# The second FFN product of each unit by Strassen's scheme, with 256-column matmuls and sums on GpSimd

## The chip, the cores and the metric

The kernel runs on one core of a Trainium2 chip. A core has a matrix engine (TensorE, PE in the profile), three engines for elementwise work (VectorE or DVE, ScalarE or ACT, GpSimd or POOL) and a queue that issues DMAs (SyncE or SP). Each engine works through its own list of instructions in order and waits on semaphores for the others. Only PE, DVE and ACT reach the accumulators (PSUM banks); POOL works on SBUF alone. The metric is the time of one execution on the device, in microseconds; lower is better.

## The reference

The inputs are q, k and v of 8 sequences, 8 heads, 576 positions and 64 features, a layer norm's gain and two FFN weights. Attention is local, in chunks of 64 positions; its output, brought to 4608 rows of 512 features, goes through a layer norm and an FFN with a residual:

```python
scores = scale * np.matmul(q_c, k_c.transpose(0, 1, 2, 4, 3))
attn = np.exp(scores - np.max(scores, axis=-1, keepdims=True))
attn = attn / (np.sum(attn, axis=-1, keepdims=True) + 1e-09)
out = np.matmul(attn, v_c)
...
xn = (x - mu) / np.sqrt(var + 1e-06) * g_ln
ch = np.maximum(xn @ w_ch1, 0.0) @ w_ch2
return x + ch
```

## The kernel before, in words

The 4608 rows are 18 pairs of 256 rows, or 9 tiles of 512. The first three tiles (pairs 0 to 5) go through attention and a plain FFN while the weights are read, rounded and split. The other six tiles form three units of two tiles (1024 rows), and a unit's FFN is `unit_ffn`.

*Precision.* Each float32 operand is split into a high part (fp32r, written by ScalarE) and a low part (the difference, by DVE or POOL). A product is three matmuls: high x high, high x low, low x high. So `m` runs over three terms everywhere.

*First product of a unit* (512 to 2048 features). It is done by Strassen's scheme: the unit's two tiles and two halves of the features give seven combinations of activations (`operand`, made by `combine`), and the weights seven combinations that `prepare` writes to DRAM (`wa`). Per quarter `q` of the hidden features there are 14 steps (seven products for two `e`), each `product` six matmuls of 512 columns (line 778). The four PSUM banks of `ps_y` hold two accumulators per `e`, `c_` and `a_`. After most steps something leaves a bank: ScalarE copies it to a snapshot or to `hu` (line 784), or DVE adds the bank and a snapshot into `hu` (line 787). `hu` holds the unit's hidden values, 2 x 16 blocks of 128 x 512.

*Second product of a unit* (2048 back to 512). It is plain: for each of the two tiles `n` and 16 blocks `f`, 12 matmuls of 512 columns (line 863: four groups of rows `j` by three terms), accumulated over `f` in four banks. Ahead of them, `split` has ScalarE write the rectified high part (line 800) and `rest` has DVE write the low part (line 805). At the end DVE adds the residual (line 903) and SP stores the rows.

*Weights.* A ring of six buffers of 512 KB each is loaded by SP (line 687): 28 loads per unit of `wa` and 32 of `w2d` (the second weight, written plainly to DRAM by `prepare`).

*Order.* Every engine's list is written out by hand. Up to the units the order comes from strings and tables of tokens: `START`, `SECOND`, `THIRD`, where one letter is one step of a stream (`S` is a step of `prepare`, `P` and `Q` are `combine` of the two halves for the first unit). In the units, `weave` counts the matmuls of 512 columns that `unit_ffn` has issued (0.2267 us each) and lets in steps of the next unit's attention and of `combine` at given counts (`PAIR_SPAN`, `STEPS`, `FIRST_HALF`, `LAST_HALF`). Attention of a pair has two blocks of small matmuls on PE (lines 298 and 387), transposes of 32 x 32 blocks on DVE (lines 358 and 467) and reductions, scalings and statistics on DVE and ScalarE. In `combine`, `part` has ScalarE write an operand's high part (line 730) and POOL its low part (line 731), and `less` subtracts on DVE (line 734).

*Preparation* (`prepare`). For each of eight pairs of weight blocks: POOL adds the high and low parts of the first weight together (line 635), makes four combinations of 256 columns (lines 643 to 646), ScalarE copies the high parts (line 655), POOL subtracts them (line 657), and SP writes all to DRAM; five steps per pair of blocks.

Of the kernel before, what the change touches and what calls it, by code (L numbers as in the profile page):

```python
# [44 lines left out]
    0: "CS", 1: "CS", 2: "DDGS", 3: "DS", 4: "DDS", 5: "DS", 6: "DGS", 7: "GGHS", 8: "DG", 9: "D", 10: "GGP",  # L45
    11: "HGGP", 12: "G", 13: "G", 14: "GGHP", 15: "GHP", 16: "GHP", 17: "GP", 18: "HHGP", 19: "HGP", 20: "HGP",
# [4 lines left out]
PAIR_SPAN = 140  # L51
LOADED = 8
STEPS = (0, 6, 11, 18, 26, 37, 48, 59, 68, 76, 88, 95, 102, 110, 118, 129, 140, 158)
ONE_STEP = 9
FIRST_HALF = 345
LAST_HALF = 592
REST = (2, 6, 20)
# [15 lines left out]
RING = 6  # L73

# [23 lines left out]
def chunk_attention_ffn(ctx: ExitStack, tc: tile.TileContext, qkv, v01, g, w, out):  # L98
# [527 lines left out]
    w2d = [dram.tile([P, 2, DM], F32, name="w2d", tag=f"w2d{f}") for f in range(NF)]  # L626

    def prepare():
        late = []
        for p in range(NF // 2):  # L630
            fe, q, e = 2 * p, p // 2, p % 2
            both = [wp[fe], wp[fe + 1]]
            t_ = raws.tile([P, 2, 2, PAIR], F32, name="sums", tag="wf")
            for i in range(2):
                nc.gpsimd.tensor_tensor(
                    out=t_[:, i], in0=both[i][:, 0, :DM].rearrange("p (a n) -> p a n", a=2).bitcast(F32),
                    in1=both[i][:, 1, :DM].rearrange("p (a n) -> p a n", a=2).bitcast(F32), op=ALU.add,
                )
            for i in range(2):
                nc.sync.dma_start(w2d[fe + i], both[i][:, :, DM:].bitcast(F32))  # L640
            yield
            a11, a12, a21, a22 = t_[:, 0, 0], t_[:, 0, 1], t_[:, 1, 0], t_[:, 1, 1]
            nc.gpsimd.tensor_tensor(out=a22, in0=a21, in1=a22, op=ALU.add)
            nc.gpsimd.tensor_tensor(out=a21, in0=a11, in1=a21, op=ALU.subtract)
            nc.gpsimd.tensor_tensor(out=a11, in0=a22, in1=a11, op=ALU.subtract)
            nc.gpsimd.tensor_tensor(out=a12, in0=a12, in1=a11, op=ALU.subtract)
            for to, of in late:
                nc.sync.dma_start(to, of.bitcast(F32))
            nc.sync.dma_start(wa[q][:, e, 0], both[0][:, :, PAIR:DM].bitcast(F32))
            nc.sync.dma_start(wa[q][:, e, 1], both[0][:, :, :PAIR].bitcast(F32))  # L650
            nc.sync.dma_start(wa[q][:, 6, e], both[1][:, :, PAIR:DM].bitcast(F32))
            yield
            yield
            r = raws.tile([P, 2, 2, 2, PAIR], F32R, name="parts", tag="raw")
            nc.scalar.copy(r[:, 0], t_)
            yield
            nc.gpsimd.tensor_tensor(out=r[:, 1], in0=t_, in1=r[:, 0].bitcast(F32), op=ALU.subtract)
            late = [
                (wa[q][:, 2 + e, 0], r[:, :, 0, 0]), (wa[q][:, 4 + e, 1], r[:, :, 0, 1]),
                (wa[q][:, 4 + e, 0], r[:, :, 1, 0]), (wa[q][:, 2 + e, 1], r[:, :, 1, 1]),  # L660
            ]
            yield
        for to, of in late:
            nc.sync.dma_start(to, of.bitcast(F32))
        yield

    class Ring:
# [10 lines left out]
        def fetch(self):  # L678
            if self.given < len(self.loads):
                place = self.places[self.given % RING]  # L680
                of = self.loads[self.given]
                to = place[:, : 2 * DM].bitcast(F32)
                if len(of.shape) == 4:
                    to = to.rearrange("p (i h n) -> p i h n", i=2, h=2)
                else:
                    to = to.rearrange("p (h n) -> p h n", h=2)
                nc.sync.dma_start(to, of)
                self.given += 1
# [8 lines left out]
    for _ in range(UNITS):  # L697
        for q in range(NF // 4):
            ring.loads.extend(wa[q][:, i] for i in range(7))
        ring.loads.extend(w2d[f][:, :, :] for _ in range(2) for f in range(NF))  # L700
# [17 lines left out]
    def operand(name):  # L718
        if name not in shared:
            shared[name] = const.tile([P, 2, 2, 2 * PAIR], F32R, name="xc", tag=f"w{'2165734'.index(name)}")  # L720
        return shared[name]

    def combine(half):
# [4 lines left out]
        def part(name, x):  # L728
            o = operand(name)[:, :, :, cs].rearrange("p h k (j t) -> p h k j t", j=2)
# [11 lines left out]
        yield  # L741
        less(b12, b22, b12)
        yield
        part("3", b22)
        yield
        less(b22, b22, b11)
        yield
        part("6", b22)
        yield
        part("5", b11)  # L750
        yield
        less(b21, b21, b22)
        yield
        part("7", b12)
# [4 lines left out]
    def unit_ffn(u):  # L759
        first = 2 * LEAD + 4 * u  # L760
        tail = u == UNITS - 1
        hu = {}
        for n in range(2):
            for f in range(NF):
                if f // 2 not in hu:
                    hu[f // 2] = shared.setdefault(
                        f"h{f // 2}", None
                    ) or const.tile([P, 2, 2, DM], F32, name="hu", tag=f"w{8 + f // 2}")
                    shared[f"h{f // 2}"] = hu[f // 2]
# [3 lines left out]
        def product(bank, w, name, start):  # L773
            x = operand(name)
# [14 lines left out]
        more = []  # L789
        order = [(n, f) for n in range(2) for f in range(NF)]  # L790
        parts = []

        def split(i):
            n, f = order[i]
            if i % 5 > 1:
                hh, hl = more[i % 5 - 2][:, 0], more[i % 5 - 2][:, 1]
            else:
                hh, hl = (hp_.tile([P, 1, DM], F32R, name=f"h{c}")[:, 0] for c in "hl")
            x = hu[f // 2][:, n, f % 2]
            nc.scalar.activation(hh, x, AF.Relu)  # L800
            parts.append((hh, hl, x))

        def rest(i):
            hh, hl, x = parts[i]
            nc.vector.scalar_tensor_tensor(  # L805
                out=hl, in0=x, scalar=0.0, in1=hh.bitcast(F32), op0=ALU.max, op1=ALU.subtract
            )

        for q in range(NF // 4):
# [8 lines left out]

            steps = []
            for e in range(2):  # L820
                steps += [
                    (c_, e, "2", None),
                    (a_, e, "1", lambda e: (copy(s[e][0], a_[e]), add(h[e][:, 0, 0], c_[e], s[e][0]))),
                ]
            for e in range(2):
                steps += [
                    (a_, e, "6", lambda e: copy(s[e][1], a_[e])),
                    (c_, e, "5", lambda e: copy(s[e][2], c_[e])),
                ]
            for e in range(2):  # L830
                steps += [
                    (a_, e, "7", lambda e: add(h[e][:, 1, 1], a_[e], s[e][2])),
                    (c_, e, "3", lambda e: add(h[e][:, 1, 0], c_[e], s[e][1])),
                ]
            for e in range(2):
# [193 lines left out]
```

## Time and profile before

| | |
|---|---|
| time, median of 3 runs | 845.76 us (845.73 to 846.2) |
| the profiled execution | 846.09 us, of which the span from the first to the last instruction is 844.3 us |
| granted TensorE clock | 0.999 |
| units start at | 326.5, 502.0 and 677.4 us |
| busy in the span | PE 831.7, weight loads 682.0, DVE 561.4, ACT 270.8, POOL 151.5 us |
| DMA | 192.6 MB, mean 228 GB/s |

Durations of a row are of a single instruction; the engines overlap the end of one with the start of the next, so that the start-to-start distance can be shorter than the duration (PE: 391 ns long, 227 ns apart). A group's row names line, engine, operation, output and inputs, shape and count, then busy time and mean duration in ns, then the idle time of the engine before them and what ended it. A row of the order of time begins with start and length in us.

### The profile page before, as it was taken

To read this page: it belongs to the slowest core of one execution; us is meant where nothing else is said; L and a number is where in the kernel's file an instruction comes from. 1 tells how busy PE (TensorE), PEld (TensorE's weight loads), DVE (VectorE), ACT (ScalarE), POOL (GpSimd) and SP (SyncE) were. 2 spreads that over 40 slices of the span, in tenths; PEclk is the share of its full clock that TensorE was granted. 3 is DMA by queue.
4 is the path that set the end of the run, shared out by engine and by line. 5 is a ranking of instruction groups with operands and counts; after the bars stand their busy time and mean duration, and the time that the engine had idled before them with its cause. 6 is when DMAs were issued, how large, how long until landed. Compare 5 with 4: busy or idle time off the path is not lost.

```text
span 844.3 us, 14613 instructions
## 1 busy us (share of the span) xinstructions
PE 831.7 (99%) x5850; PEld 682.0 (81%) x5850; DVE 561.4 (66%) x957; ACT 270.8 (32%) x425; POOL 151.5 (18%) x138
## 2 busy tenths in 40 slices
PE   7999999999999999999999999999999999999998
PEld 4888888888888888888787888887878888888886
DVE  6989966787556736797999927879999421232321
ACT  5766431122322333222341402324223212232220
POOL 0111006473751223000130400001302300000000
PEclk9999999999999999999999999999999999999999
DMA  9997417938982147776786868877658776667572
GB/s 363 328 274 221 157 43 239 345 142 286 324 270 79 42 175 259 230 257 200 254 312 208 291 190 296 276 217 254 236 192 276 243 248 188 192 195 246 189 281 106
DMA packets 69043, 192.60 MB, mean 228 GB/s; under 512 B 6640, under 2 KB 20976, under 8 KB 67056
## 3 DMA queue, kind: packets, MB, share of 16 engines
q1 hardware_dynamic: 67680, 186.95, 64.1%
q0 software_dynamic: 1296, 4.72, 2.9%
q8 instruction: 46, 0.75, 0.3%
q14 instruction: 21, 0.17, 0.1%
HBM read 147.08 MB, written 39.85 MB: 221 GB/s over the span
## 4 chain that ended last, share of the span: by engine, by line
PE 84%; DVE 11%; DMA 2%; issue 1%; ACT 1%; SPq 0%; POOL 0%; ACTq 0%; DVEq 0%; POOLq 0%
PE y L778 24%; PE y L863 17%; PE y L551 15%; PE h L527 15%; PE h L863 8%; DVE pt_sb L358 3%; DVE rows L467 2%; PE s L298 2%; DMA wp<-wfs 1%; PE h L387 1%; DVE hx L805 1%; DVE top L305 1%; DMA k_t<-qkv 1%; PE s L387 1%; DVE hu L787 1%
## 5 line engine op out<-in xcount | busy, mean ns | idle before, releaser
L778 PE MATMUL y<-xc,ring 128*128 128x512 f32 x1008 | 232.5, 391 | 0.4 <-DVE hu L787 0.4
L778 PEld LDWEIGHTS y<-xc,ring 128*128 128x128 f32 x1008 | 188.3, 188 | 40.6 <-DVE hu L787 1.2
L527 PE MATMUL h<-xth,wp 128*128 128x512 f32 (+1 forms) x432 | 129.6, 370 | 1.1 <-DMA wp<-wfs 1.1
L863 PE MATMUL y<-ring,hx 128*128 128x512 f32 x486 | 128.0, 391 | 0.0
L863 PEld LDWEIGHTS y<-ring,hx 128*128 128x128 f32 x486 | 90.8, 188 | 19.0
L787 DVE TENSOR_TENSOR hu<-y,snap 128x512 f32<-128x512 f32 x72 | 49.2, 690 | 82.8 <-ACT snap L784 43.2
L551 PE MATMUL y<-wp,hh 128*128 128x512 f32 x376 | 96.2, 394 | 0.0
L527 PEld LDWEIGHTS h<-xth,wp 128*128 128x128 f32 x432 | 78.2, 188 | 15.9 <-DMA wp<-wfs 1.3
L784 ACT COPY snap<-y 128x512 f32<-128x512 f32 x72 | 42.2, 586 | 121.2 <-PE y L778 121.2
L731 POOL TENSOR_TENSOR xc<-rows,xc 128x512 fp32r<-128x512 f32 x42 | 58.7, 1413 | 123.8 <-ACT xc L730 119.8
L551 PEld LDWEIGHTS y<-wp,hh 128*128 128x128 f32 x376 | 69.1, 188 | 13.9
L358 DVE STREAM_TRANSPOSE pt_sb<-p_sb 32x256 f32<-32x256 f32 x176 | 76.7, 436 | 3.5 <-ACT p_sb L333 0.5
L527 PE MATMUL h<-xtl,wp 128*128 128x512 f32 (+1 forms) x216 | 78.3, 367 | 0.0
L541 DVE SCALAR_TENSOR_TENSOR hl<-h,hh 128x512 fp32r<-128x512 f32 (+1 forms) x53 | 33.0, 629 | 64.9 <-ACT hh L540 64.7
L863 PE MATMUL y<-ring,hh 128*128 128x512 f32 x252 | 68.9, 389 | 0.0
L467 DVE STREAM_TRANSPOSE rows<-xg 32x256 f32<-32x256 f32 x144 | 62.7, 436 | 5.4 <-ACT xg L449 3.2
L540 ACT ACTIVATE hh<-h 128x512 fp32r<-128x512 f32 (+1 forms) x53 | 28.5, 546 | 117.7 <-PE h L527 117.7
L805 DVE SCALAR_TENSOR_TENSOR hx<-hu,hx 128x512 fp32r<-128x512 f32 x54 | 43.9, 817 | 30.2 <-PE y L863 12.2
L863 PEld LDWEIGHTS y<-ring,hh 128*128 128x128 f32 x252 | 47.3, 188 | 9.9
L551 PE MATMUL y<-wp,hl 128*128 128x512 f32 x188 | 51.8, 390 | 0.0
L437 POOL TENSOR_TENSOR rstd<-vare,mhalf 128x2 f32<-128x2 f32 x12 | 10.6, 886 | 229.5 <-DVE vare L436 229.5
L863 PE MATMUL h<-ring,hx 128*128 128x512 f32 x162 | 49.9, 389 | 0.0
(130 smaller groups left out, 986.6 us busy)
## 6 DMA issues: line engine op xcount, KB each, us to landing
ring<-w2d SPq DMA_DIRECT2D x96, 512.0 KB, 4.3
ring<-wa SPq DMA_DIRECT2D x84, 512.0 KB, 4.3
raw<-w SPq DMA_DIRECT2D x15, 1024.0 KB, 7.3
out<-x SPq DMA_DIRECT2D x36, 256.0 KB, 4.5
q_t<-qkv SPq DMA_DIRECT2D x17, 512.0 KB, 5.8
k_t<-qkv SPq DMA_DIRECT2D x17, 512.0 KB, 6.8
v_t<-qkv SPq DMA_DIRECT2D x32, 256.0 KB, 6.8
w2d<-wp SPq DMA_DIRECT2D x16, 512.0 KB, 7.1
```

The costliest lines, as they stand in the source:

```text
L358: nc.vector.transpose(out=pt_sb[quad(2 * h2 + j), :, c, quad(i)], in_=p_sb[quad(2 * c + i), :, h2, quad(j)])
L467: nc.vector.transpose(out=to[quad(j), :, quad(i)], in_=of[quad(i), :, quad(j)])
L527: nc.tensor.matmul(h, lhsT=(wh, wh, wl)[m][:, ks], rhs=(xth, xtl, xth)[m][:, k, :], start=i == 0, stop=i == len(terms) - 1,)
L540: nc.scalar.activation(hh, h, AF.Relu)
L541: nc.vector.scalar_tensor_tensor(out=hl, in0=h, scalar=0.0, in1=hh.bitcast(F32), op0=ALU.max, op1=ALU.subtract)
L551: nc.tensor.matmul(sums(pairs[j // 2])[j % 2], lhsT=(hh, hh, hl)[m], rhs=(wh, wl, wh)[m], start=f == 0 and m == 0, stop=f == NF - 1 and m ...
L731: nc.gpsimd.tensor_tensor(out=o[:, 1], in0=x, in1=o[:, 0].bitcast(F32), op=ALU.subtract)
L778: nc.tensor.matmul(bank, lhsT=w[:, (0, 0, 1)[m], ks], rhs=x[:, (0, 1, 0)[m], k, :], start=start and k == m == 0, stop=k == 1 and m == 2, s ...
L784: nc.scalar.copy(out, bank)
L787: nc.vector.tensor_tensor(out=out, in0=bank, in1=s, op=ALU.add)
L805: nc.vector.scalar_tensor_tensor(out=hl, in0=x, scalar=0.0, in1=hh.bitcast(F32), op0=ALU.max, op1=ALU.subtract)
L863: nc.tensor.matmul(ys[j], lhsT=(hh, hh, hl)[m], rhs=w[:, (0, 1, 0)[m]], start=f == 0 and m == 0, stop=f == NF - 1 and m == 2,)
```

## The change

The second product of a unit goes by Strassen's scheme too. The two tiles' hidden values and the two halves of the hidden blocks give the activations' combinations, and the second weight is split into halves of its 512 columns, so that a product has 256 columns: seven products (named in `DOWNS`, "4126573") of eight blocks `p`, each 12 matmuls of 256 columns.

- `prepare` (its rounds `c`, of a pair of blocks `p` and one of the two weights, `kind`) now also makes seven combinations of the second weight (`wb`); 16 rounds of three steps instead of eight of five. The four combinations of a round go to DVE; the sums of high and low parts and the low parts stay on POOL. `S` runs on in `THIRD` up to entry 16.
- After the steps of the first product ScalarE copies both banks (`one`, `seven`, `three`) and POOL adds the copies (`mix`); ScalarE rectifies in place three steps later (`relu`).
- POOL makes the activations' sums in `hu` (`mix_1`, `mix_2`, `mix_4`, `mix_3`).
- For each of the 56 items (a product and a block), ScalarE copies the high part (`high`) and POOL or DVE subtracts (`low`). In the first two units items 0 to 7 are subtracted on POOL, 8 to 17 on DVE, from 18 on every third and from 32 on every second on POOL; in the last unit all but the first on DVE. `high` of item i is issued at item i - 7 (i - 6 from item 40, i - 4 from item 45), `low` 0.6 items later.
- DVE adds the finished banks to the spilled rows in eight steps (`gather`); the stores of two pairs of a unit are issued in the next one.
- `combine` has another order of the same operations and operand buffers per unit; `PAIRS`, `STEPS`, `LAST_STEPS`, `COMBINE`, `LATE_COMBINE` replace the old counts. A step of six matmuls of 256 columns counts 3.17.

```diff
+    def add_up(c):
+        for i in range(2):
+            nc.gpsimd.tensor_tensor(out=sums[:, c % 2, i], in0=..., in1=..., op=ALU.add)
...
+    def combinations(c):
...
+        for out, x, y, plus in todo:
+            nc.vector.tensor_tensor(out=out, in0=x, in1=y, op=ALU.add if plus else ALU.subtract)
+    for c in range(len(chunks) + 1):
+        if c > 0:
+            nc.scalar.copy(his, t_)
+        if c < len(chunks):
+            add_up(c)
+        if c > 0:
+            nc.gpsimd.tensor_tensor(out=t_.bitcast(F32R), in0=t_, in1=his.bitcast(F32), op=ALU.subtract)
...
+        yield
...
+        yield
+        if c < len(chunks):
+            combinations(c)
+            yield
...
+    def low(i):
+        hh, hl, x = split[i]
+        share = 99 if tail else 0 if i < 8 else 99 if i < 18 else 3 if i < 32 else 2
+        engine = nc.vector if share and i % share else nc.gpsimd
+        engine.tensor_tensor(out=hl, in0=x, in1=hh.bitcast(F32), op=ALU.subtract)
...
+        at = i - (7 if i < LONG else 6 if i < LONG + 5 else 4)
+        plan += [(at, high, i), (at + 0.6, low, i)]
+    for p in range(NF // 2):
+        plan += [(2.2 + 1.2 * p, mix_2, p), (13 + 1.8 * p, mix_4, p), (22 + 1.6 * p, mix_3, p)]
...
-                (a_, e, "1", lambda e: (copy(s[e][0], a_[e]), add(h[e][:, 0, 0], c_[e], s[e][0]))),
+    def one(e):
+        copy(s[e][0], a_[e])
+        copy(h[e][:, 0, 0], c_[e])
+        mix(h[e][:, 0, 0], h[e][:, 0, 0], s[e][0], ALU.add)
+        return h[e][:, 0, 0]
...
+    def down(t, m, j):
+        name, p = items[t]
+        bank, (hh, hl) = ys["c" if name in "4253" else "a"], split[t][:2]
+        nc.tensor.matmul(
+            bank[j // 2][:, j % 2 * PAIR : (j % 2 + 1) * PAIR], lhsT=(hh, hh, hl)[m][:, j * P : (j + 1) * P],
+            rhs=loaded[t // 2][:, t % 2, (0, 1, 0)[m]], ...
+        )
```

More of the change, by code (lines that the diff above doesn't have):

```diff
@@ L803, in rest, with relu, mix @@
[L803 to L807, printed above, removed]
+        def relu(x):
+            nc.scalar.activation(x, x, AF.Relu)
+        def mix(out, x, y, op):
+            nc.gpsimd.tensor_tensor(out=out, in0=x, in1=y, op=op)
+        items = [(x, p) for x in DOWNS for p in range(NF // 2)]
+        source = {"1": (0, 0), "2": (0, 1), "6": (0, 0), "5": (1, 0), "7": (0, 0), "3": (0, 1), "4": (1, 1)}
@@ L918, in weave @@
+        if not tail:
+            shared["stores"] = [(store, 0, i, j) for i in range(2) for j in range(2)]
     def weave(ffn, side):
@@ L923, in weave @@
             while side and side[0][0] <= at:
[L924 removed]
+                _, what = side.pop(0)
+                if isinstance(what, tuple):
+                    what[0](*what[1:])
+                else:
+                    next(what)
         assert not side
```

372 lines of the change are left out of this document (201 added, 171 removed).

## The prediction

> **What bounds the kernel now.** I read the page first (span, engines, chain), then the span cut into the three units, then the chain in order of time, then the groups by line, and last the order of time of VectorE (DVE) and GpSimd (POOL) where both work.
>
> ```profile
> span 844.3 us, 14613 instructions
> PE 831.7 (99%) x5850; PEld 682.0 (81%) x5850; DVE 561.4 (66%) x957; ACT 270.8 (32%) x425; POOL 151.5 (18%) x138
> PE 84%; DVE 11%; DMA 2%; issue 1%; ACT 1%; SPq 0%; POOL 0%; ACTq 0%; DVEq 0%; POOLq 0%
> 326.50:502.00 175.50, 174.82 (x1235) 142.83 (x1234) 142.17 (x258) 53.73 (x91) 25.19 (x19) 1.00 0.72 243
> 502.00:677.40 175.40, 174.58 (x1233) 142.68 (x1232) 141.56 (x256) 53.21 (x90) 23.90 (x18) 1.00 0.73 246
> 677.40:844.30 166.90, 163.18 (x720) 134.77 (x719) 44.25 (x65) 38.49 (x64) 0.00 (x0) 0.99 0.63 208
> 126.00:270.00 144.00, 144.00 (x1234) 117.81 (x1232) 94.27 (x170) 36.85 (x55) 76.17 (x68) 1.00 0.71 245
> 395.00:460.00 65.00, 64.32 (x514) 51.93 (x513) 61.52 (x115) 21.12 (x37) 10.80 (x8) 1.00 0.71 249
> ```
>
> TensorE (PE) bounds it: 99% of the span, and 84% of the chain. The window rows give length, then busy time of PE, weight loads, DVE, ACT (ScalarE), POOL. In the first two units PE is idle by the view for under 1 us of 175; DVE works 142 of 175, and 61.5 of 65 between 395 and 460, without holding PE up by much. POOL is nearly idle there, 24 to 25 us. So the number of matmuls times their spacing is the time, and DVE is the engine with no room.
>
> **The change part by part.** *Matmuls.* The spacing is read from the chain in order of time (start, length, what):
>
> ```profile
> 63.07 4.11 PE y L551 x18
> 67.18 1.43 PE h L527 x12
> 68.61 1.39 PE y L551 x6
> ...
> 677.38 76.16 PE y L778 x336
> 753.54 43.52 PE y L863 x192
> ```
>
> 512 columns cost 43.52/192 = 0.2267 us each, 256 columns 1.43/12 = 0.119 us (a little over half). Removed per unit: 2 x 16 x 12 = 384 matmuls of 512, 87.0 us. Added: 7 products x 8 x 12 = 672 of 256, 80.1 us. Gain 6.9 us a unit, 20.8 us for three. The first product of a unit is unchanged. A sentence apart: the Trainium skill (TensorE: Matmul & The Clock Gate, Back-to-back issue gap) gives 518 cycles for 512 columns and 262 for 256, 216 and 109 ns at 2.4 GHz; by it the gain is 82.9 - 73.2 = 9.7 us a unit, but both rows lie above it, the 256 one by more, so the rows decide.
>
> *Additions out of the banks.* Six DVE additions per quarter of the first product go; instead ScalarE copies both banks and POOL adds.
>
> ```profile
> L787 DVE TENSOR_TENSOR hu<-y,snap 128x512 f32<-128x512 f32 x72 | 49.2, 690 | 82.8 <-ACT snap L784 43.2 <-PE y L778 38.9
> L784 ACT COPY snap<-y 128x512 f32<-128x512 f32 x72 | 42.2, 586 | 121.2 <-PE y L778 121.2
> L800 ACT ACTIVATE hx<-hu 128x512 fp32r<-128x512 f32 x54 | 33.2, 628 | 47.0 <-PE y L863 29.9 <-PE h L863 17.2
> L805 DVE SCALAR_TENSOR_TENSOR hx<-hu,hx 128x512 fp32r<-128x512 f32 x54 | 43.9, 817 | 30.2 <-PE y L863 12.2 <-PE h L863 12.2 <-ACT hx L800 5.4
> L635 POOL TENSOR_TENSOR sums<-wp 128x512 f32<-128x512 f32 x16 | 20.3, 1289 | 0.5
> 157.17 2.54 POOL L635 TENSOR_TENSOR sums<-wp 128x512 f32<-128x512 f32 x2
> ```
>
> Per quarter (14 steps x 6 x 0.2267 = 19 us of PE): ScalarE 14 x 0.59 + 6 x 0.63 = 12.0 us, POOL 6 x 1.25 = 7.5 us (two in 2.54 us, so 1.25 each in a row). Both fit. A bank is wanted again two steps (2.7 us) after its copy is issued, and the copies take at most 1.2 us: I cost this at nothing. Without that cover, an exponential of attention waiting on ScalarE could hold a copy up by a microsecond or two, three times a unit; I put that in the range.
>
> *Sums, splits and the port.* Before the second product's 56 operands can be used, POOL has to make 8 x 4 sums (mix 1, 2, 4, 3), and each operand needs a ScalarE copy and a subtraction of two SBUF operands, on POOL or DVE. Where POOL and DVE both read two SBUF operands, the trace shows that they take turns:
>
> ```profile
> 475.16 1.74 POOL L731 TENSOR_TENSOR xc<-rows,xc 128x512 fp32r<-128x512 f32 x1 [6.25 <-ACT xc L730]
> 480.73 4.70 POOL L731 TENSOR_TENSOR xc<-rows,xc 128x512 fp32r<-128x512 f32 x3 [3.83 <-ACT xc L730]
> 479.30 0.69 DVE L734 TENSOR_TENSOR rows<-rows 128x512 f32<-128x512 f32 x1
> 481.21 1.37 DVE L805 SCALAR_TENSOR_TENSOR hx<-hu,hx 128x512 fp32r<-128x512 f32 x1 [0.62 <-ACT hx L800]
> 482.50 1.78 DVE L734 TENSOR_TENSOR rows<-rows 128x512 f32<-128x512 f32 x1
> 484.20 1.77 DVE L805 SCALAR_TENSOR_TENSOR hx<-hu,hx 128x512 fp32r<-128x512 f32 x1
> 485.90 0.68 DVE L805 SCALAR_TENSOR_TENSOR hl<-hu,hh 128x512 fp32r<-128x512 f32 x1
> ```
>
> With POOL idle such a DVE instruction takes 0.68 or 0.69 us (about 0.61 from start to start); with POOL running its 1.25 us instructions in a row, DVE starts one every 1.70 us (482.50, 484.20, 485.90), and a POOL instruction lasts 1.74 us. A pair thus costs 1.70 us, so a DVE instruction takes 1.70 - 1.25 = 0.45 us from POOL. DVE reading a bank in PSUM (L787, 690 ns) is not of this kind.
>
> Now the demand in units 0 and 1. Take the stretch from 36 matmuls before the end of the first product to item 32 of the second. PE: 36 x 0.2267 + 32 items x 12 x 0.119 + four attention blocks of 1.09 = 58.4 us. POOL gets 29 sums and bank additions, 17 subtractions of splits (items 0 to 7, then every third, then every second) and 2 of the next unit's operands: 48 x 1.25 = 60.0 us, and two small ones of 0.7. DVE gets 22 subtractions of splits, one of the operands and 4 scalings of attention, all with two SBUF operands: 27 x 0.45 = 12.2 us of the same port. Demand 73.5 us against 58.4: 15 us behind at item 32. A split's subtraction is issued 6.4 items ahead and first used by the ninth matmul of its item, 7.07 items x 1.43 = 10.1 us of lead. So at least 15 - 10 = 5 us of stall per unit. The rest of the product gives POOL 15 and DVE 16 such instructions, 26 us in 34 us of PE, which works the backlog off, but from item 45 the lead is only 3.4 + 0.67 items, 5.8 us, so little more than that may be left.
>
> The upper end comes from DVE. Its own work in the stretch is 40 transposes x 0.45, 23 x 0.61, 8 bank reads x 0.61 and some 12 us more of attention, 49 us; if each of its 27 two-operand instructions takes 1.70 instead of 0.61, it needs 78 us for 58.4: 20 us behind, and attention's transposes, which PE's attention products wait for, are queued behind it. Bounds 5 and 20 us; I take 12 per unit, the middle, since neither row is nearer: in the 395 to 460 window DVE was as full and PE hardly stalled, while at 482 to 486 both ran at the bad pace. The page's rule, in a sentence apart: the Trainium skill (SBUF — State Buffer, Who interferes with whom) says that a DVE instruction with two SBUF inputs and a POOL instruction that reads SBUF exclude one another for the whole instruction; the trace agrees that they exclude one another, and by "whole" the 27 would cost 0.69 each, 6.5 us more.
>
> In the last unit there is no attention, nearly all splits go to DVE: 30 POOL instructions and 38 of DVE's in the stretch, 30 x 1.25 + 38 x 0.45 = 55 us in 54 us. The lead covers that: nothing.
>
> *Preparing the weights* (about 128 to 265 us). Eight rounds of five tokens become sixteen of three, about 8.7 us each, and 24 fewer POOL combinations of 256 columns stand against 64 combinations on DVE; splits and writes double.
>
> ```profile
> 177.05 2.55 POOL L635 TENSOR_TENSOR sums<-wp 128x512 f32<-128x512 f32 x2
> 174.58 2.40 POOL L657 TENSOR_TENSOR parts<-sums,parts 128x1024 fp32r<-128x1024 f32 x1 [1.95 <-ACT parts L655]
> 177.00 2.00 SPq L648 DMA_DIRECT2D wa<-parts  x4
> wa<-parts SPq DMA_DIRECT2D x32, 256.0 KB, 5.4
> DMA to landing us min/median/max: 2.1/5.4/8.1
> ```
>
> A round is: add up 2.5, subtract 2.4, issue four writes 1.5 to the last one's start, and land 2.1 to 5.4, and only then may the next round's adding up overwrite that half of the sums: 8.5 to 11.8 us against 8.7. DVE's combinations wait for the adding up, and the splits of the running product (which PE waits for) wait behind them on DVE. Bounds: 0, and 16 x 3.1 less 3 us of slack, 47 us. I take 7 us: the writes are now 128 KB each, so their landing is nearer the minimum (3 us gives a round of 9.4, 0.7 x 16 less slack), and the combinations of up to 0.4 us each can meet the 2.4 us subtraction. SP issues 11 writes a round, about 5.5 us of 8.7: no bound. Bytes written grow (56 x 256 KB instead of 16 x 512 KB), the ring's loads shrink by 4 of 60 a unit: nothing.
>
> *Moved work.* Three of the four attentions of the next unit now run beside the first product, where DVE lost 24 x 0.69 = 16.6 us; the window rows give DVE 100 us of a unit without bank additions and splits (142.2 - 16.6 - 32 x 0.8 of L805), so three attentions and the rest come to some 65 us in 83 us of PE: nothing. The fourth is spread over the second product, counted above. The spilled rows are brought back into the buffers of the last two operands; SP waits for those to be free with the ring's loads queued behind it, but the ring holds six loads (6 x 2.7 us), so nothing. Four stores of a unit go behind the first step of the next, on SP alone, whose queue has room: nothing. In the last part of the first product the operand subtractions of the second half now follow into the next unit's first steps (6 x 1.25 us on POOL, which has little else there): nothing.
>
> *The end.* The last additions are four of half the width instead of one; the store after them is half as large. Nothing.
>
> Sum against the profiled execution (846.09 us; its span 844.3): -20.8 + 2 x 12 + 7 = +10.2, 856.3 us; the median of the runs is 0.3 lower, so 856 us.
>
> **The rivals.** (1) *The port costs nothing that PE sees* (the other side): leads of 10 us hide the queues, rounds of preparation keep to 8.7 us. For it: PE lost under 1 us of 65 with DVE at 61.5. Against: the 15 us of backlog. It gives 846 - 20.8 = 825 us; it wins over "slower" once the stall is under 5 us a unit with 7 us of preparation. (2) *The stalls come at their lower ends* (5 a unit, preparation 2 to 9): -20.8 + 10 + 6 = -5, 841, near no change. (3) *Preparation becomes a chain through DMA*: with the median landing of 5.4 us, +25 to +47 instead of +7: 875 us and more. For it: those 5.4 us; against: smaller writes.
>
> **How the numbers follow.** Forecast 0.55 (846 to 868), rival 1 0.2, rival 2 0.13, rival 3 0.12. Faster by over 0.2% (about 1.7 us, what a measurement here can tell): rival 1 and most of 2, with a little of the forecast's edge, 0.30. Same: 0.05. Slower: 0.65. The range for 8 in 10 runs from 829 (half of rival 1 out) to 874 (rival 3 out).
>
> **What would show it.** Matmuls of 256 columns 0.119 us apart; POOL busy without gaps through most of the second product of units 0 and 1, its instructions 1.25 or 1.7 us; DVE's subtractions of 1.2 to 1.8 us instead of 0.69; PE waits on hl and hx from POOL and DVE, 8 to 16 us a unit, units of 178 to 183 us, the last one about 160; the first unit starting some 7 us later than 326.5. The prediction is wrong if PE shows no such waits (units of 169 us), or if the first unit starts at 345 or later.

## The result: slower by 3.55%

The changed kernel takes 874.61 us, median of 4 runs (873.15 to 879.96), against 845.75 us (844.62 to 846.2) before: a ratio of 1.0355, 95% interval 1.031 to 1.04. The prediction was 856 us, range 829 to 874: the direction is right, the loss is 29 us instead of 10, and the time lies 0.6 us above the range. The profiled execution is the longest of the four, 879.96 us.

The page of the changed kernel: span and engines.

```profile
span 878.2 us, 17196 instructions
PE 833.4 (95%) x6714; PEld 723.7 (82%) x6714; DVE 671.2 (76%) x998; ACT 396.9 (45%) x649; POOL 484.1 (55%) x349
```

PE fell from 99% busy to 95%, POOL's work tripled, and DVE's rose by 110 us. The span of the changed kernel cut into the stretch ahead of the units and the three units (length; busy time of PE, weight loads, DVE, ACT, POOL; granted clock; DMA):

```profile
126.00:356.10 230.10, 214.26 (x1616) 174.29 (x1616) 181.66 (x297) 62.00 (x91) 110.76 (x74) 0.95 0.62 213
356.10:536.70 180.60, 172.37 (x1522) 154.43 (x1521) 154.02 (x238) 90.74 (x159) 133.06 (x96) 0.98 0.68 225
536.70:717.30 180.60, 172.44 (x1523) 154.52 (x1522) 155.53 (x240) 92.04 (x162) 138.34 (x100) 0.98 0.69 229
717.30:878.20 160.90, 156.95 (x1010) 143.62 (x1008) 75.76 (x78) 80.53 (x141) 92.91 (x63) 0.99 0.63 205
```

and the first of these stretches before the change, from the same view:

```profile
126.00:326.40 200.40, 200.40 (x1607) 164.33 (x1606) 129.41 (x232) 53.53 (x84) 93.35 (x83) 1.00 0.61 213
```

Read by stretch, the 33.9 us between the two spans are +29.7 ahead of the units, +5.2 in each of the first two units (180.6 for 175.4) and -6.2 in the last (160.9 for 167.1). Here a unit begins with its first matmul, which puts the three units before the change at 326.4, 501.7 and 677.2. The stretch ahead of the units is the surprise, for none of its matmuls was changed. PE is busy there 200.4 of 200.4 us before; afterwards it is idle for 230.10 - 214.26 = 15.8 us, and the same matmuls keep it busy 13.9 us longer, at a granted clock of 0.95 instead of 1.00. Two profiles below, of kernels with this preparation unchanged, start the first unit at 350.4 and 351.2, so 24 to 25 us is the usual loss here; 24.5 + 2 x 5.2 - 6.2 = 28.7 is close to the 28.9 between the medians. The same preparation thus put the first unit at 350.4, 351.2 and 356.1; a place of the first unit, read from one execution, says little about differences of a few microseconds.

What PE waited for in that stretch and, behind the dots, in the first unit (engine, line, releaser: us in total, times, longest):

```profile
PE h L390 <- DVE hl L544: 11.0, 3, 4.6
PE y L554 <- DVE hl L544: 4.6, 1, 4.6
...
PE y L984 <- POOL hx L856: 3.3, 3, 1.5
PE y L984 <- POOL hl L856: 2.3, 1, 2.3
PE h L390 <- DVE pt_sb L361: 1.9, 2, 1.5
PE y L984 <- DVE hx L856: 0.3, 2, 0.2
```

Four waits, all for a split `hl` (line 544) that DVE writes for the product running then, cost 15.6 us. One of them in the order of time of the changed kernel (start, length; the four engines' rows were read one after the other):

```profile
285.05 7.20 DVE L361 STREAM_TRANSPOSE pt_sb<-p_sb 32x256 f32<-32x256 f32 x16
292.29 3.94 DVE L682 TENSOR_TENSOR sums<-sums 128x256 f32<-128x256 f32 x4
296.15 0.68 DVE L544 SCALAR_TENSOR_TENSOR hl<-h,hh 128x512 fp32r<-128x512 f32 x1
...
293.08 2.87 POOL L657 TENSOR_TENSOR sums<-wp 128x512 f32<-128x512 f32 x2 [0.40 <-DMA wb<-sums]
...
289.76 0.60 ACT L543 ACTIVATE hh<-h 128x512 fp32r<-128x512 f32 x1 [4.33 <-PE h L530]
...
296.88 1.97 PE L390 MATMUL h<-v_t,pt_sb 64*64 64x64 f32 x60 [4.24 <-DVE hl L544]
298.79 3.78 PE L554 MATMUL y<-wp,hh 128*128 128x512 f32 x8
```

The high part of the split is ready at 290.4 (ACT, 289.76 + 0.60), but on DVE the low part stands behind the transposes and four combinations of the weight sums (line 682). These take 3.94 us together, beside POOL's next sums (line 657), and PE stands still from 292.6 to 296.9. And then its eight matmuls at 298.79 take 3.78 us, 0.47 each, where twice 0.2267 would be 0.453.

### The profile page after: what moved, and what is told of

The parts are those of the page before. It is cut to its first block, busy times and chain, and to the rows that moved or that the text cites. A ratio compares the mean times of both kernels' runs of the same rounds, so it can differ in the third digit from the quotient of the medians.

```text
span 878.2 us, 17196 instructions
## 1 busy us (share of the span) xinstructions
PE 833.4 (95%) x6714; PEld 723.7 (82%) x6714; DVE 671.2 (76%) x998; ACT 396.9 (45%) x649; POOL 484.1 (55%) x349
## 5 line engine op out<-in xcount | busy, mean ns | idle before, releaser
L811 PEld LDWEIGHTS y<-xc,ring 128*128 128x128 f32 x1008 | 188.1, 188 | 39.4
L984 PE MATMUL y<-ring,hx 128*128 128x256 f32 x1440 | 181.9, 285 | 7.5 <-POOL hx L856 6.6
L984 PEld LDWEIGHTS y<-ring,hx 128*128 128x128 f32 x1440 | 176.8, 193 | 10.4 <-POOL hx L856 8.5
L826 POOL TENSOR_TENSOR hu<-hu 128x512 f32<-128x512 f32 x96 | 148.8, 1574 | 4.9 <-DVE hx L856 4.9
L826 POOL TENSOR_TENSOR hu<-hu,snap 128x512 f32<-128x512 f32 x72 | 93.6, 1303 | 99.4 <-ACT hu L817 97.9
L856 DVE TENSOR_TENSOR hx<-hu,hx 128x512 fp32r<-128x512 f32 x86 | 109.6, 1307 | 6.3 <-ACT hx L850 4.1
L850 ACT CAST hx<-hu 128x512 fp32r<-128x512 f32 x120 | 72.1, 619 | 79.5 <-PE y L984 54.5
L554 PE MATMUL y<-wp,hh 128*128 128x512 f32 x376 | 100.5, 407 | 0.0
L856 DVE TENSOR_TENSOR hl<-hu,hh 128x512 fp32r<-128x512 f32 x31 | 37.2, 1214 | 72.3 <-ACT hh L850 72.2
L554 PEld LDWEIGHTS y<-wp,hh 128*128 128x128 f32 x376 | 71.9, 196 | 15.0
L767 POOL TENSOR_TENSOR xc<-rows,xc 128x512 fp32r<-128x512 f32 x42 | 57.9, 1389 | 35.3 <-ACT xc L766 33.9
L657 POOL TENSOR_TENSOR sums<-wp 128x512 f32<-128x512 f32 x32 | 42.2, 1338 | 39.4 <-DMA wb<-sums 23.0
```

The source lines that it names most:

```text
L554: nc.tensor.matmul(sums(pairs[j // 2])[j % 2], lhsT=(hh, hh, hl)[m], rhs=(wh, wl, wh)[m], start=f == 0 and m == 0, stop=f == NF - 1 and m ...
L657: nc.gpsimd.tensor_tensor(out=sums[:, c % 2, i], in0=both[i][:, 0, cols].rearrange("p (a n) -> p a n", a=2).bitcast(F32), in1=both[i][:, 1 ...
L767: nc.gpsimd.tensor_tensor(out=o[:, 1], in0=x, in1=o[:, 0].bitcast(F32), op=ALU.subtract)
L811: nc.tensor.matmul(bank, lhsT=w[:, (0, 0, 1)[m], ks], rhs=x[:, (0, 1, 0)[m], k, :], start=start and k == m == 0, stop=k == 1 and m == 2, s ...
L826: nc.gpsimd.tensor_tensor(out=out, in0=x, in1=y, op=op)
L850: nc.scalar.copy(hh, split[i][2])
```

## The experiments

**Ahead of the units.** Theory A: the 64 combinations on DVE stand in the way of the splits; A1, because they wait in the queue for sums; A2, because they do not get through beside a running POOL instruction. Rival B: the rounds themselves are late, because POOL may form the next sums only when the writes have landed, which was the prediction's reason for its upper bound. The four runs that tell these apart, and a fifth for a remedy:

*No combinations.*

```diff
         if c < len(chunks):
-            combinations(c)
             yield
```

> The 64 combinations of the weight sums on VectorE are left out (so the weights of the products 2, 4, 5, 6, 7 are plain sums); GpSimd's sums and low parts, ScalarE's copies and all writes stay. Theory A (the combinations, 45.3 us of VectorE in the stretch before the units and each of them waiting for GpSimd, stand in VectorE's queue ahead of the splits hl that TensorE waits for): the stalls of 16.4 us and the slow clock behind them go, the first unit starts at 326 to 332 instead of 356.1, time 845 to 852. Theory B (the rounds themselves are late, because GpSimd waits 39.3 us for writes to land before it may form the next sums): the first unit stays at 348 or later, time 866 or more. Theory C (VectorE's other work is slowed by GpSimd's use of the shared port): half of it stays, first unit 338 to 345.

*Combinations as one-input instructions.*

```diff
-            nc.vector.tensor_tensor(out=out, in0=x, in1=y, op=ALU.add if plus else ALU.subtract)
+            nc.vector.transpose(out=out, in_=x)
```

> Each combination (two inputs, 0.36 to 2.60 us) becomes a VectorE transpose of the same 128x256 tile (one input; 0.435 us for the 32x256 ones of the trace), at the same place in the queue and with the same waits; the weights of those products come out wrong. Theory A split in two. A1 (what delays the splits is that a combination waits in the queue for GpSimd's sums): as the changed kernel, first unit at 350 to 357, time 868 to 875. A2 (what delays them is that a two-input combination does not get through beside a running GpSimd instruction, 3.75 to 5.23 us for four that take 1.5 us alone): first unit at 328 to 338, time 846 to 857. Theory B (landing): 348 or later.

*Combinations on GpSimd.*

```diff
-            nc.vector.tensor_tensor(out=out, in0=x, in1=y, op=ALU.add if plus else ALU.subtract)
+            nc.gpsimd.tensor_tensor(out=out, in0=x, in1=y, op=ALU.add if plus else ALU.subtract)
```

> The 64 combinations go back to GpSimd, where the kernel before had its 32 (0.74 to 0.78 us each): 64 x 0.75 = 48 us more on GpSimd, which was busy about 42.2 + 39.5 + some 30 us of 215 in this stretch, and VectorE loses 45.3 us. Theory A: the first unit starts at 326 to 334, time 845 to 853, if GpSimd's longer rounds (2 x 1.3 + 2.4 + 4 x 0.75 = 8.0 us of the 8.7 between rounds) still keep up. Theory B (the chain of a round with its landing is what is late): the chain is 2 us longer than with VectorE, first unit at 356 or later, time 874 or more.

*Second writes not from the sums.*

```diff
-            write((target(*chunks[c - 1], at)[:, 1], t_[:, at[1], at[2]]))
+            write((target(p, kind, at)[:, 1], wp[2 * p][:, 1, left]))
```

> The second write of each place (the low part) takes its data from the weight tile instead of the tile of sums, so that GpSimd's next sums need not wait for that write to land; the low parts in memory are then wrong, the numbers of instructions and bytes the same. Theory B (landing): GpSimd's 39.3 us of waits before its sums mostly go, the rounds come back to 8.7 us, first unit at 328 to 338, time 846 to 857. Theory A (VectorE's queue): the combinations still collide with GpSimd and still stand ahead of the splits, first unit at 350 to 357, time 868 to 875.

*Low part ahead of the next sums.*

```diff
+        if c > 0:
+            nc.gpsimd.tensor_tensor(out=t_.bitcast(F32R), in0=t_, in1=his.bitcast(F32), op=ALU.subtract)
         if c < len(chunks):
             add_up(c)
         if c > 0:
-            nc.gpsimd.tensor_tensor(out=t_.bitcast(F32R), in0=t_, in1=his.bitcast(F32), op=ALU.subtract)
             for at in places(*chunks[c - 1]):
```

> Ahead of the units, GpSimd does the low part of the last round (2.47 us) before the two sums of the next one, not behind them, so that GpSimd has nothing to do when VectorE's four combinations come; nothing is left out. Theory A2 (combinations are slow because a GpSimd instruction runs beside them): four combinations come to 1.5 to 2.0 us from a mean of 2.8, the stalls of 4.4 to 4.8 us go, first unit at 331 to 340, time 849 to 859. Rival (the order on GpSimd puts the low part, which waits for ScalarE's copy, in front of the sums, so each round is a chain of 0.4 x 4 + 1.05 + 2.4 + 2.6 us through three engines and VectorE waits at its head): combinations fast but later, first unit at 345 to 356, time 863 to 875.

What was measured, by where the first unit starts (the kernel before: 326.4; the changed one: 350.4 to 356.1). "Idle" is the window's length less PE's busy time, "slower" is that busy time less 200.4:

| run | first unit | PE idle | PE slower | median | ratio to before (95%) |
|---|---|---|---|---|---|
| no combinations | 330.8 | 2.3 | 2.1 | 853.11 | 1.0083 (1.0059 to 1.0107) |
| as transposes | 332.1 | 4.2 | 1.6 | 855.84 | 1.0122 (1.0097 to 1.0147) |
| on GpSimd | 342.4 | 9.9 | 6.1 | 863.07 | 1.0204 (1.0173 to 1.0235) |
| no landing | 345.1 | 12.7 | 6.0 | 870.1 | 1.0288 (1.0263 to 1.0313) |
| low part first | 342.5 | 10.2 | 5.9 | 867.94 | 1.0263 (1.0235 to 1.0291) |

The rows behind it are the windows of each of the five runs, in this order:

```profile
126.00:330.80 204.80, 202.47 (x1608) 165.76 (x1607) 135.96 (x233) 61.43 (x91) 108.46 (x74) 0.99 0.70 239
```

```profile
126.00:332.10 206.10, 201.95 (x1605) 164.19 (x1604) 157.24 (x297) 61.70 (x90) 109.05 (x74) 1.00 0.70 238
```

```profile
126.00:342.40 216.40, 206.51 (x1607) 167.82 (x1606) 137.83 (x233) 60.49 (x91) 156.22 (x138) 0.98 0.67 226
```

```profile
126.00:345.10 219.10, 206.40 (x1600) 166.59 (x1599) 177.81 (x294) 61.42 (x90) 110.63 (x74) 0.97 0.66 224
```

```profile
126.00:342.50 216.50, 206.30 (x1604) 166.84 (x1603) 167.50 (x297) 61.41 (x90) 109.71 (x74) 0.98 0.66 226
```

The run without combinations puts the first unit where A has it (its time, 853.11, is 1 us over the expected), and theory C of its expectation, 338 to 345, is out with it. The transposes decide between A1 and A2. They stand at the same places, wait for the same sums, and DVE still has 157 us of work; yet the first unit starts at 332.1, 1.3 us behind the run with nothing there at all. The groups of lines 682 and 657 in this stretch say why. In the changed kernel:

```profile
L682 DVE TENSOR_TENSOR sums<-sums 128x256 f32<-128x256 f32 x64 | 45.3, 708 | 3.4 <-POOL sums L657 1.6
L657 POOL TENSOR_TENSOR sums<-wp 128x512 f32<-128x512 f32 x32 | 42.2, 1338 | 39.4 <-DMA wb<-sums 23.0 <-DMA wa<-sums 16.3
```

and with transposes:

```profile
L682 DVE STREAM_TRANSPOSE sums<-sums 128x256 f32<-128x256 f32 x64 | 24.5, 422 | 4.0 <-POOL sums L657 3.3
L657 POOL TENSOR_TENSOR sums<-wp 128x512 f32<-128x512 f32 x32 | 41.0, 1304 | 39.5 <-DMA wb<-sums 24.3 <-DMA wa<-sums 15.1
```

64 instructions at 422 ns beside the same POOL work, where the two-input ones average 708 ns and reach 2.60 us. And POOL waits for the writes as long as in the changed kernel, 39.5 us against 39.4, while nearly all of the loss is gone: the wait for landing does not make the loss by itself. In the run without landing, B's quantity does vanish: POOL's idle time ahead of its sums falls from 39.4 us to 0.7, while the combinations stay at 708 ns.

```profile
L682 DVE TENSOR_TENSOR sums<-sums 128x256 f32<-128x256 f32 x64 | 45.3, 708 | 2.5 <-POOL sums L657 0.7
L657 POOL TENSOR_TENSOR sums<-wp 128x512 f32<-128x512 f32 x32 | 42.0, 1333 | 0.7
```

It gives back 5 to 11 us of the 24 to 30, A2's removal 18 to 24. So B is a part of it and no more: 345.1 lies between its forecast (328 to 338) and theory A's (350 to 357), and fits neither. Two more expectations missed on both sides. On GpSimd (342.4, between 334 and 356) the combinations no longer collide, but ACT's copy `his` is queued directly behind them, and everything behind that copy waits; in its view of waits:

```profile
ACT his L687 <- POOL sums L682: 43.3, 10, 6.9
```

With the low part first (342.5, between 340 and 345), the combinations run at 509 ns, and both halves of the expectation come true at once: they are fast, and they wait for sums that come later.

**In the units.** Theory P: DVE's two-input instructions and POOL's pass one at a time, and that is what the second product waits for. Rival Q: POOL alone is late.

*Subtractions of the first two units as ScalarE copies.*

```diff
+        if share and i % share and not tail:
+            nc.scalar.copy(hl, x)
+            return
```

> In the first two units the subtractions for hx that VectorE does (23 a unit at 1.35 us) become ScalarE copies, so that the low parts there are wrong; GpSimd's 25, its mixes and everything in the last unit and ahead of the units stay. Theory P (VectorE's two-input instructions and GpSimd's get through one at a time, and that serial pair is what the second product waits for): both become faster, GpSimd's mixes come to 1.3 us from 1.53, TensorE's waits of 4.2 us a unit on hl and hx and most of the rest of the distance between 180.6 and the 160.9 of the last unit go; units 166 to 172, time 848 to 858. Rival Q (GpSimd alone is late, being busy 133 us of 180.6 a unit with ScalarE in between, and the attention for the next unit on VectorE costs the rest): units 177 to 181, time 868 to 875.

*The token combinations as well.*

```diff
     def less(out, x, y):
+        if u > 0:
+            nc.scalar.copy(out, x)
+            return
         nc.vector.tensor_tensor(out=out, in0=x, in1=y, op=ALU.subtract)
```

> As the run with ScalarE copies for the subtractions of the first two units, and the token combinations of the second and third unit (line 770, 8 a unit) are ScalarE copies too, so nothing that VectorE does in a unit but the 8 centrings of line 446 takes two inputs from SBUF; those operands and low parts are wrong. Theory P (one at a time, and in that run a single combination stood 14.04 us behind 11 GpSimd instructions in a row): the 11 us waits go with it, nothing of size is left, units at 166 to 171, time 846 to 856. Rival Q (GpSimd alone, or ScalarE with 54 copies more): units at 177 or more, time 868 or more.

The first of the two took 876.56 us (ratio 1.0364, 1.0339 to 1.0389), units of 181.6 and 181.3: by its number, nearer to rival Q. (DVE has 31 such subtractions a unit; the 23 of the expectation are those that write `hx`.) Its trace says otherwise. No wait for `hx` or `hl` is left; in its place stands one wait of 10.8 us in each unit, and the order of time shows what was running:

```profile
459.95 14.04 DVE L770 TENSOR_TENSOR rows<-rows 128x512 f32<-128x512 f32 x1 [7.76 <-POOL xc L767]
474.00 1.81 DVE L361 STREAM_TRANSPOSE pt_sb<-p_sb 32x256 f32<-32x256 f32 x4
...
459.87 1.29 POOL L859 TENSOR_TENSOR hl<-hu,hh 128x512 fp32r<-128x512 f32 x1
...
470.96 2.47 POOL L826 TENSOR_TENSOR hu<-hu 128x512 f32<-128x512 f32 x2
```

A single two-input DVE instruction, 0.69 us by itself, lasts 14.04 us. It begins just behind the first of 11 POOL instructions that follow one another without a gap, and it ends 0.6 us after the last of them; attention's transposes, which PE waits for, stand behind it. So the experiment had not removed the conflict: it had left the eight token combinations of a unit, and one of them was enough. The second run takes those out too: 853.98 us (ratio 1.0093, 1.007 to 1.0115), and its windows of the first two units are

```profile
351.20:520.90 169.70, 167.97 (x1522) 151.72 (x1522) 117.09 (x200) 109.85 (x199) 122.09 (x97) 1.00 0.71 243
520.90:690.60 169.70, 167.90 (x1522) 151.63 (x1521) 117.99 (x200) 110.69 (x201) 124.94 (x100) 1.00 0.72 242
```

with as many instructions on POOL as before and ACT 19 us busier. The unit falls from 180.6 to 169.7 us, and Q is out: POOL alone keeps up, and its sums in `hu` (line 826 of the changed kernel) take 1.34 us on the mean of the second unit where they took 1.53. Some of the conflict is left even here, in an instruction with a single input, which takes 0.17 us by itself:

```profile
462.05 12.55 DVE L369 TENSOR_SCALAR den<-den 128x16 f32<-128x16 f32 x1
```

It lasts until ten POOL instructions without a gap between them are through (the second unit has another, of 12.60 us), but nothing that PE needs soon stands behind it: PE's waits add up to 1.7 and 1.8 us in these two units. The 10.9 us are not the conflict's alone, since DVE is also rid of 39 x 0.69 = 27 us of work of its own (31 subtractions and 8 combinations); the first run of the next group, which leaves DVE that work, helps to separate the two.

**A version that works.** The remaining four runs ask whether the same work can be placed so that it does not collide.

*Units retimed* (on top of the low part first): fewer subtractions on POOL, the last quarter's additions for products 7 and 3 back on DVE out of the bank, other times.

```diff
-PAIRS = (6, 116, 226, 340)
+PAIRS = (6, 116, 226, 325)
...
-        share = 99 if tail else 0 if i < 8 else 99 if i < 18 else 3 if i < 32 else 2
+        share = 99 if tail else 0 if i < 8 else 99 if i < 32 else 4 if i < 42 else 99
...
+            if q == NF // 4 - 1:
+                add(h[e][:, 1, 1], a_[e], s[e][2])
+                return h[e][:, 1, 1]
```

> The order of the run before this one, and the units' instructions given out at other times: VectorE takes the subtractions of items 8 to 31 alone and GpSimd a quarter of items 32 to 41 (17 and 9 fewer for GpSimd than of items 18 to 55 now), the last quarter's sums of products 7 and 3 go back to VectorE straight from the bank, mixes and attention steps are moved by a few microseconds; nothing is left out. By theory P GpSimd's load in the second product is what counts, and it falls by some 15 x 1.47 = 22 us a unit: units 170 to 176, time 9 to 21 less than that of the run before. If the port's sum of both is what counts, whoever does the work: units 178 to 182, no gain.

*Steps of the sums elsewhere in the order ahead of the units* (on top of the units retimed; `THIRD` is changed in the same way).

```diff
-    0: "ABS", 1: "AS", 2: "S", 3: "AAS", 4: "AS", 5: "AS", 6: "AS", 7: "AS", 8: "AAS", 9: "AAS", 10: "AAS", ...
+    0: "ABS", 1: "AS", 2: "S", 3: "AAS", 4: "A", 5: "ASS", 6: "AS", 7: "AS", 8: "AAS", 9: "AA", 10: "AASS", ...
```

> The retimed run with the steps of the weight sums handed out at other places of the order ahead of the units: each round's steps are moved by one or two places (13 of 50), so that a round's combinations stand behind the splits that TensorE waits for and not ahead of them; work and units as in that run, where the first unit starts at 344.2 and a unit takes 173.9. If the place in VectorE's queue is what is left of the delay: first unit at 329 to 336, time 840 to 847. If VectorE's load itself is (about 120 of 144 us busy): 340 or later, time 850 or more.

*Every second pair of rounds on GpSimd* (on top of the run before, with the steps at other places again).

```diff
+            engine = nc.gpsimd if c % 4 > 1 else nc.vector
...
-                nc.vector.tensor_tensor(out=out, in0=x, in1=y, op=ALU.add if plus else ALU.subtract)
+                engine.tensor_tensor(out=out, in0=x, in1=y, op=ALU.add if plus else ALU.subtract)
```

> As the run before this one, with the combinations of every second pair of rounds on GpSimd (32 of 64 at 0.757 us, 24 us more there, 16 us less on VectorE) and the steps at places fitted to that. GpSimd's busy share stays under 70% ahead of the units, VectorE's load falls by 16 us. By queue place and load alike: first unit at 328 to 334, time 838 to 846; if GpSimd's longer rounds are late instead: 338 or later, time 848 or more.

*Units once more* (on top of the run before; the times of the mixes and of the token combinations change too).

```diff
-        share = 99 if tail else 0 if i < 8 else 99 if i < 32 else 4 if i < 42 else 99
+        share = 99 if tail else 0 if i < 8 else 99 if i < 9 else 99 if i < 35 else 2
-        at = (-6.0, -4.6, -4.3, -3.9, -3.0, -1.8, -0.5, 0.2)[i]
+        at = (-9.9, -8.8, -5.8, -4.9, -2.9, -2.9, -0.1, 0.2)[i]
...
```

> As the run before this one, with the units' order changed once more: VectorE takes the subtractions of items 8 to 34 alone, then every second one, the first eight begin 1 to 4 matmul groups earlier, the mixes and the token combinations are spread differently. By theory P a unit gains what VectorE and GpSimd no longer need of the port at the same time: units 170 to 173, time 3 to 8 below the run before; if the remaining waits of a unit (9 of 0.3 to 1.5 us on subtractions) are set by the mixes' chain through GpSimd: no change within 2 us.

| run | first unit | its length | median | ratio to before (95%) |
|---|---|---|---|---|
| units retimed | 344.2 | 173.8 | 853.98 | 1.0093 (1.0071 to 1.0115) |
| steps elsewhere | 337.4 | 173.8 | 845.63 | 0.9997 (0.9981 to 1.0013) |
| half on GpSimd | 336.0 | 174.0 | 845.15 | 0.999 (0.9976 to 1.0004) |
| units once more | 333.6 | 173.7 | 844.31 | 0.9978 (0.9964 to 0.9991) |

Retiming brought 13.96 us over the run that it builds on, within its 9 to 21, nearly all of it from units of 173.8 us instead of 180.6. DVE is as busy there as in the changed kernel, and POOL less so:

```profile
518.00:692.00 174.00, 170.08 (x1523) 152.19 (x1522) 155.64 (x257) 90.36 (x158) 113.54 (x82) 1.00 0.71 236
```

155.6 us of DVE against 155.5, 113.5 of POOL against 138.3. DVE even has more subtractions, 45 in this unit at 0.96 us on the mean, where 31 took 1.33: it is the meeting of the two that was shortened, not DVE's load, and 6.8 of the 10.9 us went with it. The run changed several things at once, and only together with the run before it, where POOL alone kept up, does it single out the meeting. Moving the steps brought the first unit to 337.4, 1.4 us short of what the place in the queue was to give; with half of the combinations on GpSimd it is 336.0, 2 short of the expected; both times were in their ranges. That the second of these steps gained anything is not shown: 845.63 and 845.15 us are each within the other's runs. The last change did nothing to a unit, as its rival said; with the same preparation as the run before, its first unit starts 2.4 us earlier all the same, which is within what one preparation scatters, and its median is 0.84 us lower. Its windows:

```profile
126.00:333.60 207.60, 202.95 (x1606) 165.14 (x1605) 144.56 (x265) 60.93 (x90) 132.68 (x106) 0.99 0.69 236
333.60:507.30 173.70, 168.66 (x1522) 151.74 (x1521) 155.37 (x249) 89.59 (x155) 117.52 (x85) 1.00 0.70 236
507.30:681.10 173.80, 169.85 (x1523) 153.09 (x1522) 156.95 (x251) 91.01 (x158) 122.23 (x89) 0.99 0.70 236
681.10:842.00 160.90, 156.94 (x1010) 143.62 (x1008) 72.83 (x82) 78.44 (x137) 86.09 (x59) 1.00 0.63 205
```

The whole change, placed like this, is 0.22% faster than the kernel before and 30 us faster than as it was made. Of the 20.8 us that the matmuls save, 7.2 go back ahead of the units and up to 4 in each of the first two units (173.7 less 169.7) to what is left of the conflict and to DVE's own work.

## Why the prediction came out wrong

**The step that failed is "Preparing the weights", taken at +7 us.** It measured 24 to 30. Its bounds of 0 and 47 hold that, and the remark that "the combinations of up to 0.4 us each can meet the 2.4 us subtraction" names the mechanism; but the price was worked out from the landing of writes alone, and the collision got no term of its own, although the pair of 1.70 us in the quoted order of time was at hand to price it. The landing itself was sized well. It was taken at 3 us, and the changed kernel's list of DMA issues (last column, median us to landing) has

```profile
wa<-sums SPq DMA_DIRECT2D x32, 128.0 KB, 3.2
wb<-sums SPq DMA_DIRECT2D x32, 128.0 KB, 1.8
```

With the wait for it gone, 5 to 11 us came back, about the 7 foreseen; the 18 to 24 that came back with the collision stood at nothing. Sixteen rounds by four combinations at 708 ns instead of 422 is 18 us more on DVE, in front of splits with hardly any lead. (By the groups before the change GpSimd gives up 32 combinations, not 24; no term rests on that.) In the prediction's own terms, a first unit at 345 or later was to prove it wrong, and it started at 356.1 (350.4 and 351.2 in the two other profiles).

**A term was missing: PE's clock after a wait.** The prediction counted waits only. Up to 13.9 us of the loss ahead of the units is PE working slower behind them, nearly as much as the 15.8 us of idle time. The first unit has 4.4 us of it: the same 1522 matmuls keep PE busy for 172.37 us at a granted clock of 0.98, and for 167.97 at 1.00 in the run without token combinations.

**Rival 3 had the time and not the reason.** It gave 875 us for a chain through DMA. With the wait for landing gone, the first unit still started at 345.1.

**The units were right in their sum, for the reason given, and with some luck in the size.** The prediction had -6.9 for the matmuls and +12 for the port, +5.1; measured were +5.2. The 12 were the middle of 5 and 20, with no row nearer to either; what was measured is 8.2 us of idle time, against 0.7 before, and the 4.4 of slower work, which had no term. With the conflict taken out (and part of DVE's own work with it) a unit falls by 10.9, to 169.7, against 175.4 - 6.9 = 168.5. The last unit was to lose 6.9 and lost 6.2. The chain of the changed kernel gives the difference:

```profile
717.43 76.19 PE y L811 x336
793.62 80.64 PE y L984 x672
```

80.64/672 is 0.120 us for 256 columns, where the prediction took 0.119 from a group of 12: 0.7 us a unit. Right too were POOL's and DVE's durations, in the groups of the changed kernel:

```profile
L826 POOL TENSOR_TENSOR hu<-hu 128x512 f32<-128x512 f32 x96 | 148.8, 1574 | 4.9 <-DVE hx L856 4.9
L856 DVE TENSOR_TENSOR hx<-hu,hx 128x512 fp32r<-128x512 f32 x86 | 109.6, 1307 | 6.3 <-ACT hx L850 4.1
```

DVE's subtractions average 1.31 us (1.2 to 1.8 foreseen). The waits on `hx` and `hl` are smaller than the 8 to 16 us foreseen, 5.9 us in the first unit by the view of waits; 1.9 more is the wait for attention's transposes, and the slower clock makes up the rest. The bank additions, the moved attention, the stores and the end, all taken at nothing, show in no wait of PE.

The Trainium skill (SBUF — State Buffer, Who interferes with whom) says that a DVE instruction with at most one SBUF input, outside the modes that use both port pairs, does not contend with GpSimd, and that one with two contends with a GpSimd instruction that reads SBUF; the 422 ns of the transposes beside the 708 ns of the combinations agree. The 12.55 us of line 369 do not go by the number of inputs alone, and whether that instruction ran in such a mode the trace does not tell.

## What to carry to other kernels

Before moving elementwise work to a second engine, list which of its instructions share a resource with the first, and price each meeting from a row where the two already meet; do so in every stage the change touches, also the one whose own matmuls stay as they are. Then ask what stands behind the slowed instruction in its queue: 18 us more on an engine that was 65% busy stopped PE four times, because each time the one instruction that PE waited for was behind it. And where an experiment is to remove a conflict, look in its trace for what it has left: one instruction was enough to hold PE up for 10.8 us.

## What the hardware showed that was not expected

*Waits of PE cost twice.* The changed kernel around the wait shown above: the wait, and the two stretches behind it.

```profile
292.50:296.90 4.40, 0.16 (x7) 0.03 (x5) 4.30 (x6) 0.60 (x1) 3.05 (x3) 0.93 0.60 209
297.00:302.50 5.50, 5.50 (x69) 4.61 (x70) 5.26 (x8) 0.35 (x1) 2.37 (x1) 0.50 0.56 193
302.50:308.00 5.50, 5.50 (x25) 4.52 (x24) 4.96 (x11) 1.38 (x3) 0.90 (x2) 0.95 0.54 193
```

After 4.2 us without work PE is granted half its clock for 5.5 us. Shorter waits can do it too, and need not. In the last run a wait of 1.79 us, followed by 60 small matmuls of attention, has 3.5 us at 0.55 behind it; in the run before it a longer one, of 1.94 us before the same 60 matmuls, has none (granted clock 1.00). The two waits and the stretches behind them, in this order:

```profile
188.42 1.15 PE L383 MATMUL h<-v_t,pt_sb 64*64 64x64 f32 x60 [1.79 <-DVE hl L537]
189.40:192.90 3.50, 3.50 (x19) 2.64 (x11) 3.29 (x7) 1.04 (x1) 1.54 (x1) 0.55 0.44 155
278.93 1.15 PE L383 MATMUL h<-v_t,pt_sb 64*64 64x64 f32 x60 [1.94 <-DVE hl L537]
279.00:282.50 3.50, 3.50 (x71) 3.02 (x72) 3.29 (x6) 1.05 (x1) 2.26 (x3) 1.00 0.16 55
```

Of two equal waits of 2.39 us in the last run, one in each of the first two units, only the second has a slow stretch behind it (3.5 us at 0.54). So the length of a wait does not decide by itself; what else does was not tried.

The Trainium skill (TensorE: Matmul & The Clock Gate, Part 1: The HAM clock gate) says that TensorE falls to half its clock after an idle window of about 3.4 us; the half rate agrees, but here waits of 1.79 and 2.39 us were enough in one place each.

*Taking turns is not certain.* Everywhere else in these traces a two-input DVE instruction waits for one POOL instruction and then gets through. The 14.04 us of line 770, and the same again in the second unit of that run (14.05), waited for a whole row of them, and so did the single-input instruction of line 369 in the run without token combinations (12.55 and 12.60 us). What made the difference was not tried and stays open.
